# Corner scores and cross-chunk products of a decayed attention: both heads' 128 rows contracted against zeros, in place of 64 rows of each head

## Chip, cores and metric

One core of a Trainium2 chip (8 cores in 2 dies) runs the whole kernel. The metric is the device time of one execution in microseconds, taken as the median of several runs.

## The reference

Attention without softmax, with a decay per head, and then two pairs of dense layers (with a leaky activation in the first, a GELU-like one in the second). Everything is float32.

```
batch, n_heads, seq, head_dim = (4, 8, 576, 64)
...
scores = scale * np.matmul(q, k.transpose(0, 1, 3, 2))
gamma = 1.0 - 2.0 ** (-5.0 - np.arange(H, dtype=np.float32))
rel = pos[:, None] - pos[None, :]
Dmat = np.where(rel >= 0, gamma[:, None, None] ** rel[None, :, :], 0.0)
ret = scores * Dmat[None, :, :, :]
return np.matmul(ret, v).astype(np.float32)
...
x = np.ascontiguousarray(attn_out.transpose(0, 2, 1, 3)).reshape(B * S, H * D)
x = _moe_ref(x=x, **moe_kwargs)        # (max(h, 0) + alpha * min(h, 0)) @ w_out, h = x @ w_in
return _moe2_ref(x=x, **moe2_kwargs)   # (h * sigmoid(1.702 h)) @ w_out
```

## The kernel before, in words

The attention stands at the start and the dense layers fill the rest. A unit of attention is one of 16 pairs `(b, p)`: batch `b` and two heads. The two heads lie above each other in the 128 partitions: head `e = 0` has rows 0 to 63, head `e = 1` rows 64 to 127 (`halves` holds the two slices). The 576 positions are cut into four chunks of 128 and a corner of 64. Scores are computed inside a chunk only; what earlier chunks give to later ones goes through a running 64 x 64 state of each head (a sum of outer products of keys and values), since the decay is a power.

`tc.manual_schedule()` means that each engine executes its instructions in the order in which the code calls them. The loop runs `i` from 0 to 16, and `j = i - 1` is the pair before. What one turn of it puts on TensorE (PE), all through the helper `mm` on line 353, is:

1. `a_scores(i)`, tile `sc`: 8 products that contract 64 rows into 128 columns of the array. `k[j][o]` and `q[j][o]` are one head's rows.
2. `a_outer(i)`, tile `st` from `kts` (keys by position, scaled beforehand by ScalarE in `a_keys`): 8 products that contract 128 rows into 64 columns, the two heads in different columns.
3. `a_within(j)`, tile `av` from `r` and `ld`: 8 products, 128 rows into 64 columns.
4. `a_tail(i)`, tile `st` from `ld`: the corner's scores, 2 products of 64 rows into 64 columns (for `i = 0` they stand between 1 and 2).
5. `a_across(j)`, tile `av`: 8 products of the states with the faded queries and 2 of the corner, 64 rows into 64 columns.

Each float32 product makes two records of a weight load and a matmul, so a group of 8 shows as x16. The trace writes the shape as rows * columns: 64\*128, 128\*64, 64\*64.

The other engines in a turn:

- GpSimd (POOL) multiplies the queries with a fade: `a_queries(i)`, line 400, one 128 x 448 product of two SBUF operands into `r`. A dependency added by hand lets it start only behind the instruction that `latest[0]` names, mostly the last one of `a_sums` (line 424) of the pair before.
- VectorE (DVE): `a_evac(i)`, line 385, two 128 x 512 products that read the scores from PSUM and write `r`; after it, in some turns, tables (line 335, in turns 0 to 2) or work on the dense layers' weights (lines 148, 108, 178) that `run_to` calls by a table of times; then `a_sums(i)`, lines 414, 419, 424, on the states. The last of these writes the masked corner scores back into `r`.
- ScalarE (ACT): `a_states(i)` and `a_keys(i + 1)` on line 317, copies of results (line 103), and weight work (lines 133, 137, 141).
- SyncE (SP) issues the loads: `a_load` (tile `ld`, 128 x 1728 numbers a pair, line 309, and `kts`, line 311) four to five turns ahead, weights (`raw`), stores.

SBUF is cut by hand into slots `w0` to `w15`. `TMP` gives the slots that tiles take in turn: `ld` has five, `r` two, `xs` (results on their way to DRAM) four, `w14` the last of these.

After the loop the first dense layer starts at once: `mm1` (line 514, tile `h`), then `activate`, `split` (ScalarE's and VectorE's halves of `gsf`), `mm2` (line 555, tile `acc`).

## Time and profile before

| | |
|---|---|
| runs | 800.33, 802.6, 804.19 us, median 802.6 |
| profiled execution | 800.28 us, of which the span of the instructions 798.6 |
| busy | PE 793.6 us, DVE 642.1, ACT 527.9, POOL 83.5 |
| granted clock of TensorE | 1.00 in the whole span |
| attention on PE | from 4.5 to 66.5 us of the span |

The profiled execution lies 2.3 us under the median of the runs. The trace gives start and duration of each instruction in us from the span's start, with the idle time ahead of it in brackets and what ended it ("issue" is a pause that no semaphore explains). PEld is the weight load that runs beside the matmuls. A matmul's end is modelled, so what counts on PE is how far apart the starts lie.

### The profile page before, as it was taken

Reading aid. Unit: us, or ns where it says so; the run is one execution under the profiler, and the core shown is the slowest. Engines: PE = TensorE matmul, PEld = TensorE weight load, DVE = VectorE, ACT = ScalarE, POOL = GpSimd, SP = SyncE. Lnnn points to the kernel's source line nnn. Section 1 sums busy time; section 2 is a strip of 40 time slices with the busy share of each in tenths; the row PEclk is TensorE's granted clock in tenths of the full one; section 3 lists DMA queues with packets and bytes.
Section 4 is the critical chain, followed back from the end, with each engine's and each line's share of the span. In section 5 each row is a group of like instructions: output and inputs, shape, how many; then the busy total and the mean of one; then the engine's idle time right before and its main releaser. Section 6 shows DMA issues by size and latency. Waiting matters only on the chain.

```text
span 798.6 us, 14132 instructions
## 1 busy us (share of the span) xinstructions
PE 793.6 (99%) x5004; PEld 740.2 (93%) x5004; DVE 642.1 (80%) x1195; ACT 527.9 (66%) x959; POOL 83.5 (10%) x104
## 2 busy tenths in 40 slices
PE   9999999999999999999999999999999999999998
PEld 8998888888888888999999999999999999999997
DVE  7888987888467576879999899799677898787775
ACT  7689869885536856556678666676566675666552
POOL 2230112100022003626100000000000000000000
PEclk9999999999999999999999999999999999999999
DMA  9998999755889966797989556986435985536771
GB/s 351 417 386 333 327 352 342 286 217 209 294 278 401 360 224 227 253 337 254 337 323 355 177 174 233 343 295 235 147 125 193 323 312 187 159 120 232 267 278 60
DMA packets 87789, 214.08 MB, mean 268 GB/s; under 512 B 7971, under 2 KB 43811, under 8 KB 79014
## 3 DMA queue, kind: packets, MB, share of 16 engines
q1 hardware_dynamic: 80784, 187.99, 65.6%
q0 software_dynamic: 6784, 25.17, 9.0%
q8 instruction: 39, 0.64, 0.3%
q14 instruction: 32, 0.26, 0.1%
q10 hardware_dynamic: 150, 0.02, 0.0%
HBM read 152.59 MB, written 60.56 MB: 267 GB/s over the span
## 4 chain that ended last, share of the span: by engine, by line
PE 98%; DMA 1%; DVE 0%; issue 0%
PE acc L696 33%; PE h L696 25%; PE acc L555 16%; PE h L514 16%; PE av L353 4%; PE sc L353 2%; PE st L353 2%; DMA ws<-sm 1%; PE wps L942 0%; PE dq L326 0%; DVE c L178 0%; DVE wz L930 0%
## 5 line engine op out<-in xcount | busy, mean ns | idle before, releaser
L108 DVE TENSOR_TENSOR gsf<-g,gsf 128x384 fp32r<-128x384 f32 (+1 forms) x272 | 156.4, 586 | 54.5 <-ACT gsf L103 53.1
L103 ACT ACTIVATE gsf<-g 128x384 fp32r<-128x384 f32 (+1 forms) x272 | 145.8, 542 | 75.6 <-PE acc L696 32.8
L555 PE MATMUL acc<-gsf,wo 128*128 128x512 f32 x576 | 138.2, 389 | 0.0
L514 PE MATMUL h<-x,wi 128*128 128x512 f32 x576 | 138.2, 389 | 0.0
L696 PE MATMUL acc<-gsf,ws 128*128 128x384 f32 x768 | 135.1, 334 | 0.2 <-DMA ws<-sm 0.2
L696 PEld LDWEIGHTS acc<-gsf,ws 128*128 128x128 f32 x768 | 133.2, 188 | 0.5 <-ACT x L103 0.5
L555 PEld LDWEIGHTS acc<-gsf,wo 128*128 128x128 f32 x576 | 108.1, 188 | 22.8 <-ACT raw L103 0.3
L514 PEld LDWEIGHTS h<-x,wi 128*128 128x128 f32 x576 | 108.1, 188 | 22.5
L696 PE MATMUL acc<-x,ws 128*128 128x384 f32 x660 | 128.3, 334 | 0.0
L696 PEld LDWEIGHTS acc<-x,ws 128*128 128x128 f32 x660 | 115.5, 188 | 0.2 <-ACT tm L103 0.2
L696 PE MATMUL h<-x,ws 128*128 128x384 f32 x540 | 107.7, 334 | 0.0
L696 PE MATMUL h<-gsf,ws 128*128 128x384 f32 x576 | 101.9, 334 | 0.0
L696 PEld LDWEIGHTS h<-gsf,ws 128*128 128x128 f32 x576 | 100.0, 188 | 0.2 <-issue 0.2
L696 PEld LDWEIGHTS h<-x,ws 128*128 128x128 f32 x540 | 94.8, 188 | 0.0
L178 DVE TENSOR_TENSOR tm<-h,tm 128x384 f32<-128x384 f32 x97 | 53.6, 553 | 26.9 <-PE h L696 21.5
L178 DVE TENSOR_TENSOR g<-g 128x384 f32<-128x384 f32 x114 | 63.0, 553 | 0.7
L103 ACT ACTIVATE tm<-acc 128x384 f32<-128x384 f32 x62 | 30.4, 491 | 48.0 <-PE acc L696 46.4
L522 DVE SCALAR_TENSOR_TENSOR g<-g,rise_sb,h 128x512 f32<-128x512 f32 (+1 forms) x49 | 36.4, 742 | 29.7 <-ACT g L527 29.5
L527 ACT ACTIVATE g<-h 128x512 f32<-128x512 f32 (+1 forms) x49 | 29.1, 593 | 40.5 <-PE h L514 39.9
L178 DVE TENSOR_TENSOR raw<-raw 128x256 f32<-128x256 f32 x116 | 45.6, 433 | 1.0
L148 DVE SCALAR_TENSOR_TENSOR raw<-raw 128x1024 int32<-128x1024 int32 x32 | 39.3, 1229 | 2.6 <-ACT raw L141 2.6
L129 POOL DMA_DIRECT2D raw<-in_w_dram x44 | 23.2, 534 | 173.2 <-DVE raw L178 52.9
(104 smaller groups left out, 922.9 us busy)
## 6 DMA issues: line engine op xcount, KB each, us to landing
ws<-sm SPq DMA_DIRECT2D x32, 1024.0 KB, 7.0
ws<-sp SPq DMA_DIRECT2D x24, 1024.0 KB, 5.5
raw<-in_w_dram POOLq DMA_DIRECT2D x44, 512.0 KB, 7.5
sm<-raw SPq DMA_DIRECT2D x32, 512.0 KB, 4.3
pad<-rg SPq DMA_DIRECT2D x48, 256.0 KB, 2.7
ld<-in_qkv_dram SPq DMA_DIRECT2D x13, 864.0 KB, 7.9
raw<-in_w_dram SPq DMA_DIRECT2D x20, 512.0 KB, 8.9
r<-raw SPq DMA_DIRECT2D x16, 512.0 KB, 2.9
```

Of the source, the lines that this page charges most:

```text
L103: return nc.scalar.activation(out=out, in_=in_, func=ACTF.Copy)
L108: latest[0] = eng.tensor_tensor(out=out, in0=a, in1=b.bitcast(F32), op=ALU.subtract)
L129: eng.dma_start(out=raws[key][:, c * DM:c * DM + DM], in_=f[:, c * DM:c * DM + DM])
L148: latest[0] = nc.vector.scalar_tensor_tensor(out=g[:, 0:2 * DM], in0=t[:, :, 1], scalar=3, in1=t[:, :, 0], op0=ALU.logical_shift_left, op1 ...
L178: latest[0] = (eng or nc.vector).tensor_tensor(out=out, in0=x, in1=y, op=op)
L353: return nc.tensor.matmul(out=out, lhsT=lhsT, rhs=rhs, start=start, stop=stop, skip_group_check=True)
L514: nc.tensor.matmul(out=t, lhsT=w[:, cw, k * 128:k * 128 + 128], rhs=x[:, cx], start=(i == 0), stop=(i == 3 * NK - 1),)
L522: nc.vector.scalar_tensor_tensor(out=g[0], in0=g[1], scalar=rise_sb[:, m:m + 1], in1=h, op0=ALU.mult, op1=ALU.add)
L527: nc.scalar.activation(out=out, in_=in_, func=ACTF.Relu, scale=-1.0)
L555: nc.tensor.matmul(out=acc[0][d], lhsT=w[:, d // 2, cw, d % 2 * 128:d % 2 * 128 + 128], rhs=g[:, cx], start=(m == m0 and i == 0), stop=(m ...
L696: nc.tensor.matmul(out=out, lhsT=w(cw), rhs=x(cx), start=(start and n == 0), stop=True, skip_group_check=True,)
```

## The change

The products of `a_tail` and `a_across` now contract all 128 rows of both heads. One of the two operands has zeros in the other head's rows, so the sum is the same. For that:

- the corner's keys come from the host as 128 columns with zeros (`last`), so `ld` is 128 x 1792 numbers and the loads' cuts shift by 64 columns;
- a fixed tile `rq` in slot `w14` holds the faded queries and the masked corner scores, two buffers of `[128, 2, 512]`; its other-head halves are set to zero once, by two DVE instructions at the start;
- `a_queries` is now two POOL products of 64 partitions each, and the last instruction of `a_sums` two DVE products of 64 partitions each, since each head's half goes to another column range of `rq`;
- the fourth slot of `xs` is `w3` (free of `ld` after pair 11) in place of `w14`.

```diff
-TMP = {"ld": (2, 3, 4, 5, 10), "r": (6, 7), "xs": (11, 12, 13, 14)}
+TMP = {"ld": (2, 3, 4, 5, 10), "r": (6, 7), "xs": (11, 12, 13, 3)}
...
-        t = tmp("ld", i, [128, 1728])
-        cuts = {0: (0, 512, 1152, 1728), 1: (0, 1152, 1728), 2: (0, 1152, 1728)}.get(i, (0, 1728))
+        t = tmp("ld", i, [128, 1792])
+        cuts = {0: (0, 512, 1216, 1792), 1: (0, 1216, 1792), 2: (0, 1216, 1792)}.get(i, (0, 1792))
...
-        k = [t[:, j:j + 128] for j in (128, 256, 832, 960)] + [t[:, 1088:1152]]
-        ld[i] = q, k, t[:, 1152:1728].rearrange("p (n d) -> p n d", n=9), t[:, 384:832]
+        k = [t[:, j:j + 128] for j in (128, 256, 832, 960)]
+        k.append(t[:, 1088:1216].rearrange("p (e n) -> p e n", e=2))
+        ld[i] = q, k, t[:, 1216:1792].rearrange("p (n d) -> p n d", n=9), t[:, 384:832]
...
-        for o in halves:
-            mm(s_t[i][o, 0:64], k[4][o], q[4][o], i == 0, True)
+        for e, o in enumerate(halves):
+            mm(s_t[i][o, 0:64], k[4][:, e], q[4], i == 0, True)
...
-            r[:, 1088:1600].rearrange("p (b n) -> p b n", b=2)[:, :, 0:64], r[:, 1600:2048],
-        )
-        ins = nc.gpsimd.tensor_tensor(
-            out=r_t[i][3], in0=ld[i][3], in1=tab_sb[:, PAIRS[i][1], 320:768], op=ALU.mult
-        )
-        if behind:
-            tc.add_manual_dep(ins.ins, behind.ins.name, SYNC, reason="beside the products of the scores")
+            r[:, 1088:1600].rearrange("p (b n) -> p b n", b=2)[:, :, 0:64], rq[:, i % 2],
+        )
+        for e, o in enumerate(halves):
+            ins = nc.gpsimd.tensor_tensor(
+                out=r_t[i][3][o, e, 0:448], in0=ld[i][3][o], in1=tab_sb[o, PAIRS[i][1], 320:768],
+                op=ALU.mult,
+            )
+            if behind:
+                tc.add_manual_dep(
+                    ins.ins, behind.ins.name, SYNC, reason="beside the products of the scores"
+                )
...
-        latest[0] = nc.vector.tensor_tensor(
-            out=s[:, 0:64], in0=s[:, 0:64], in1=tab_sb[:, p, 256:320], op=ALU.mult
-        )
+        for e, o in enumerate(halves):
+            latest[0] = nc.vector.tensor_tensor(
+                out=r_t[i][3][o, e, 448:512], in0=s[o, 0:64], in1=tab_sb[o, p, 256:320], op=ALU.mult
+            )
...
-            for o in halves:
-                mm(out[c][o], s[o, s0:s0 + 64], q[o, c * 128 - 128:min(c * 128, 448)], False, True)
-        for o in halves:
-            mm(out[4][o], v[o, 8], s[o, 0:64], False, True)
+            for e, o in enumerate(halves):
+                mm(out[c][o], s[:, s0:s0 + 64], q[:, e, c * 128 - 128:min(c * 128, 448)], False, True)
+        for e, o in enumerate(halves):
+            mm(out[4][o], v[:, 8], q[:, e, 448:512], False, True)
...
+        rq = wp.tile([128, 2, 2, 512], F32, tag="w14", name="rq")
+        for e, o in enumerate(halves):
+            nc.vector.memset(rq[o, :, 1 - e], 0.0)
...
+    last = np.zeros((B, NP, 128, 128), np.float32)
+    for e in range(2):
+        o = slice(64 * e, 64 * e + 64)
+        last[:, :, o, o] = kt[:, :, o, 512:]
```

How it moves instructions. On PE, turn 2 of the loop reads before and after as follows (the sizes are those of the output; `sc` are scores, `st` states and corner scores, `av` results):

```order
L353 MATMUL sc<-ld 128x128 x8
L353 MATMUL st<-ld,kts 64x64 x8
L353 MATMUL av<-r,ld 64x128 x8
L353 MATMUL st<-ld 64x64 x2
L353 MATMUL av<-r 64x128 x6
L353 MATMUL av<-r 64x64 x2
L353 MATMUL av<-r,ld 64x64 x2
```

```order
L354 MATMUL sc<-ld 128x128 x8
L354 MATMUL st<-ld,kts 64x64 x8
L354 MATMUL av<-r,ld 64x128 x8
L354 MATMUL st<-ld 64x64 x2
L354 MATMUL av<-rq,r 64x128 x6
L354 MATMUL av<-rq,r 64x64 x2
L354 MATMUL av<-rq,ld 64x64 x2
```

Number, order and output sizes are the same; the last four groups change only what they contract.

On DVE, turns 1 and 2 before and after, each with the semaphores that an instruction waits for:

```order
L385 TENSOR_TENSOR r<-sc,tab_sb 128x512 [waits PE_49] x2
L335 SCALAR_TENSOR_TENSOR tab_sb<-fade_sb,vtab_sb,mask_sb 128x128 x2
L335 SCALAR_TENSOR_TENSOR tab_sb<-fade_sb,vtab_sb,mask_sb 64x64 x2
L414 SCALAR_TENSOR_TENSOR r<-r,vtab_sb 128x192 [waits Activation_49]
L419 SCALAR_TENSOR_TENSOR r<-r,vtab_sb 128x128 [waits DVE_49]
L424 TENSOR_TENSOR r<-r,tab_sb 128x64
L385 TENSOR_TENSOR r<-sc,tab_sb 128x512 [waits PE_49,Pool_49]
L385 TENSOR_TENSOR r<-sc,tab_sb 128x512 [waits PE_49]
```

```order
L386 TENSOR_TENSOR r<-sc,tab_sb 128x512 [waits PE_49] x2
L336 SCALAR_TENSOR_TENSOR tab_sb<-fade_sb,vtab_sb,mask_sb 128x128 x2
L336 SCALAR_TENSOR_TENSOR tab_sb<-fade_sb,vtab_sb,mask_sb 64x64 x2
L419 SCALAR_TENSOR_TENSOR r<-r,vtab_sb 128x192 [waits Activation_49]
L424 SCALAR_TENSOR_TENSOR r<-r,vtab_sb 128x128 [waits DVE_49]
L430 TENSOR_TENSOR rq<-r,tab_sb 64x64 x2
```

One 128 x 64 product has become two of 64 x 64, and the first evacuation no longer waits for POOL, which no longer writes `r`.

On POOL, the queries' products of pairs 2 to 6 before, and of pairs 2 to 4 after:

```order
L400 TENSOR_TENSOR r<-ld,tab_sb 128x448 [waits DVE_49,PE_49,DMAHW1_49,Activation_49,Pool_49]
L400 TENSOR_TENSOR r<-ld,tab_sb 128x448 [waits DVE_49,PE_49,DMAHW4_49,Activation_49,Pool_49]
L400 TENSOR_TENSOR r<-ld,tab_sb 128x448 [waits DVE_49,DMAHW6_49,PE_49,Pool_49]
L400 TENSOR_TENSOR r<-ld,tab_sb 128x448 [waits DVE_49,PE_49,DMAHW1_49,Activation_49,Pool_49]
L400 TENSOR_TENSOR r<-ld,tab_sb 128x448 [waits DVE_49,PE_49,DMAHW3_49,Activation_49,Pool_49]
```

```order
L402 TENSOR_TENSOR rq<-ld,tab_sb 64x448 [waits DVE_49,PE_49,DMAHW1_49,Activation_49,Pool_49]
L402 TENSOR_TENSOR rq<-ld,tab_sb 64x448 [waits PE_49,Pool_49]
L402 TENSOR_TENSOR rq<-ld,tab_sb 64x448 [waits DVE_49,PE_49,DMAHW4_49,Activation_49,Pool_49]
L402 TENSOR_TENSOR rq<-ld,tab_sb 64x448 [waits PE_49,Pool_49]
L402 TENSOR_TENSOR rq<-ld,tab_sb 64x448 [waits DVE_49,DMAHW6_49,PE_49,Pool_49]
L402 TENSOR_TENSOR rq<-ld,tab_sb 64x448 [waits PE_49,Pool_49]
```

Each product has become two; what the second waits for is the use of its half of the buffer two pairs earlier, not the first.

## Rows read from the trace of the kernel before

**Rows 1.** The page: busy time of PE; the chain that ended last, by engine.

```profile
PE 793.6 (99%) x5004; PEld 740.2 (93%) x5004; DVE 642.1 (80%) x1195; ACT 527.9 (66%) x959; POOL 83.5 (10%) x104
...
PE 98%; DMA 1%; DVE 0%; issue 0%
```

**Rows 2.** Waits of 0 to 70 us: total us, times, longest.

```profile
PEld st L353 <- issue: 2.6, 15, 0.2
```

**Rows 3.** PE in turn 12 (timeline: start us, us, shape, xcount).

```profile
49.47 1.16 PE L353 MATMUL sc<-ld 64*128 64x128 f32 x16
...
52.06 0.33 PE L353 MATMUL st<-ld 64*64 64x64 f32 x4
52.22 0.94 PE L353 MATMUL av<-r 64*64 64x128 f32 x16
...
53.21 0.38 PE L353 MATMUL sc<-ld 64*128 64x128 f32 x2
```

**Rows 4.** PE around 51.15 and around 52.05 us alone, same columns.

```profile
50.96 0.29 PE L353 MATMUL st<-ld,kts 128*64 128x64 f32 x4
51.08 0.28 PE L353 MATMUL av<-r,ld 128*64 128x128 f32 x2
...
51.85 0.28 PE L353 MATMUL av<-r,ld 128*64 128x128 f32 x2
52.06 0.27 PE L353 MATMUL st<-ld 64*64 64x64 f32 x1
```

**Rows 5.** DVE and POOL in turn 12, timeline, idle before and its releaser in brackets.

```profile
49.40 0.42 DVE L414 SCALAR_TENSOR_TENSOR r<-r,vtab_sb 128x192 f32<-128x192 f32 x1 [1.11 <-ACT r L317]
...
50.12 0.22 DVE L424 TENSOR_TENSOR r<-r,tab_sb 128x64 f32<-128x64 f32 x1
...
50.60 1.15 POOL L400 TENSOR_TENSOR r<-ld,tab_sb 128x448 f32<-128x448 f32 x1 [2.67 <-DVE r L424]
50.74 1.29 DVE L385 TENSOR_TENSOR r<-sc,tab_sb 128x512 f32<-128x512 f32 x2 [0.39 <-PE sc L353]
...
51.94 1.22 DVE L148 SCALAR_TENSOR_TENSOR raw<-raw 128x1024 int32<-128x1024 int32 x1
```

**Rows 6.** The start: POOL's and DVE's memsets, DVE's tables, POOL's first product.

```profile
0.31 0.10 POOL L1153 MEMSET const-float32-0.0<- 128x1 f32 x1 [0.31 <-issue]
0.34 0.10 POOL L1153 MEMSET const-float32-1.0<- 128x1 f32 x1
...
0.90 0.17 DVE L930 MEMSET wz<- 128x128 f32 x1 [0.90 <-PEq L1153]
...
5.32 1.10 DVE L335 SCALAR_TENSOR_TENSOR tab_sb<-fade_sb,vtab_sb,mask_sb 128x128 f32<-128x128 f32 x4 [4.13 <-ACT fade_sb L103]
...
7.83 1.98 DVE L335 SCALAR_TENSOR_TENSOR tab_sb<-fade_sb,vtab_sb,mask_sb 128x128 f32<-128x128 f32 x4
...
8.22 1.21 POOL L400 TENSOR_TENSOR r<-ld,tab_sb 128x448 f32<-128x448 f32 x1 [6.85 <-ACT tab_sb L103]
...
11.90 1.09 DVE L335 SCALAR_TENSOR_TENSOR tab_sb<-fade_sb,vtab_sb,mask_sb 128x128 f32<-128x128 f32 x4
```

**Rows 7.** Loads: page's issues; busy by stretch (DMA share, GB/s last); turns 3 and 4.

```profile
ld<-in_qkv_dram SPq DMA_DIRECT2D x13, 864.0 KB, 7.9
...
12.00:16.00 4.00, 4.00 (x78) 3.64 (x80) 3.92 (x12) 2.75 (x9) 1.21 (x2) 1.00 1.02 416
...
15.64 1.16 PE L353 MATMUL sc<-ld 64*128 64x128 f32 x16
16.02 0.91 ACT L317 ACTIVATE kts<-kts,vtab_sb 128x256 f32<-128x256 f32 x2 [0.57 <-DMA kts<-in_kn_dram]
...
19.61 1.16 PE L353 MATMUL sc<-ld 64*128 64x128 f32 x16
```

**Rows 8.** Start of the dense layers: the lower half of `gsf`, and the products that use it.

```profile
74.31 0.68 DVE L108 TENSOR_TENSOR gsf<-g,gsf 128x512 fp32r<-128x512 f32 x1
...
74.76 2.94 PE L555 MATMUL acc<-gsf,wo 128*128 128x512 f32 x12
```

More of the change, by code (lines that the diff above doesn't have):

```diff
@@ L1115, in _layout @@
         [
-            qt[..., :128], kt[..., :256], qt[..., 128:], kt[..., 256:], vv, vt,
+            qt[..., :128], kt[..., :256], qt[..., 128:], kt[..., 256:512], last, vv, vt,
         ],
```

## The prediction

> **What bounds the kernel now.** I read the page first, then the waits, then the timeline. TensorE is busy for 793.6 of 798.6 us, and the chain that ended last is 98% TensorE [rows 1]. So time is won only by shortening what TensorE does or by taking out pauses between its instructions, and lost wherever something new comes too late for it. The list of waits holds one entry for TensorE inside the attention that repeats: ahead of the corner scores (`st`) its weight loads stand idle 15 times, 2.6 us together, with no semaphore behind it [rows 2]. That pause comes from the array itself.
>
> The timeline of one turn tells what it is. A turn lasts 53.21 - 49.47 = 3.74 us [rows 3]. Inside a group, instructions come in pairs, one for each head, and two heads share a start. Between the states (128\*64) and the products inside a chunk (128\*64) nothing happens: from 50.96, two pairs of 64 columns take 0.12 us, 0.06 each, and then the next group starts [rows 4]. The last pair of 128 columns starts at 51.85; seven pairs lie between it and 51.08, so a pair takes 0.11 us. But the corner scores (64\*64) start only at 52.06, 0.21 us later: 0.10 us more than a pair needs [rows 4]. Their own two pairs then take 52.22 - 52.06 = 0.16 us where the states' two take 0.12: another 0.04 [rows 3, 4]. So going from 128\*64 to 64\*64 costs TensorE 0.14 us. Where the shape stays, from corner scores to the products across chunks, there is no idle time.
>
> **The change, part by part.**
>
> *The pause.* All that a turn does behind its scores now has the shape 128\*64, so one of its three changes of shape is gone; the ones into and out of the scores (64\*128) stay. It is removed in 17 places: once in each of the 17 turns. All 17 give 17 x 0.14 = 2.4 us; I take fewer, below.
>
> *The products themselves.* Their number, their columns and their weight loads' columns are as before; only rows of zeros are added. The 128\*64 rows show 0.06 us for a pair of 64 columns and 0.11 for 128 [rows 4], and the products across chunks, 64\*64 so far, go at the same pace: six pairs of 0.11 and two of 0.06 make 0.78 us, and their row has 0.94 with the length of the last one [rows 3]. Cost nothing.
>
> *The loads.* `ld` grows from 864 KB a pair [rows 7] by 64 x 4 x 128 bytes = 32 KB, 16 times. In this stretch the DMA engines are full: share 1.02, 416 GB/s [rows 7]. More bytes are therefore later bytes, 0.08 us a pair, 1.3 us by the last. Where that meets TensorE is turn 3: ScalarE stood idle 0.57 us for the keys of that turn, which come last in the queue behind four loads, and turn 3 took 19.61 - 15.64 = 3.97 us instead of 3.74 [rows 7]. Four loads are 131 KB, 0.32 us. So turn 3 comes 0.32 us later, and whatever turns 0 to 2 won is lost in the same wait. Behind turn 3 the distance between landing and use grows, since later loads are issued about four turns ahead (four turns are 15 us) with a median of 7.9 us to landing [rows 7]; I price the rest at nothing, and at 1.3 us if that cover is gone.
>
> *VectorE.* The two memsets of `rq` write 1024 numbers a partition each. One of 128 took 0.17 us [rows 6], so 1.3 us each at the most; they lie in the 4.13 us in which VectorE waits for the tables' input [rows 6]: nothing. The corner scores' masking becomes two instructions in place of one of 0.22 us [rows 5]: 0.22 us more a turn at the most. Cover: in turn 12 VectorE idles 0.39 us and the sums end at 50.34, 1.9 us before the products across chunks start at 52.22 [rows 3, 5]. In turns 1 to 3 VectorE is full (3.92 of 4 us [rows 7]), and it falls 0.7 us behind there at the most, less than the 1.9. Nothing; 16 x 0.22 = 3.5 us if none of it were covered.
>
> *GpSimd.* This is the term with the widest bounds. One product of 128 x 448 took 1.15 us [rows 5]; no row shows one of 64 partitions. It may cost half (0.58) or the same (1.15), and the two may run one after the other or side by side: 1.15 to 2.30 us a turn. It matters because of VectorE. Where a GpSimd product ran beside the tables, which read two operands from SBUF, the four tables took 1.98 us against 1.10 and 1.09 without it [rows 6]. Beside the evacuation, which reads PSUM, nothing was lengthened: 1.29 us with GpSimd on top of it [rows 5]. At 1.15 us the pair stays in the shadow of the evacuation, as now; at 2.30 the second half falls on what follows, in turn 12 an instruction of 1.22 us [rows 5].
> The Trainium skill, "GPSIMD Engine Reference", section "Instruction dispatch", says that each of GpSimd's cores serves 16 partitions and starts the next instruction as soon as its own share of the last is done. By that rule the two halves, on different partitions and with no wait on each other, take about 1.15 us together; in turn they would take 2.30.
> What the rows can say points the same way: two memsets of 0.10 us start 0.03 us apart [rows 6], so GpSimd does begin an instruction before the last has ended. I take 1.15 to 1.3 us, hence no cost, and keep 2.30 as a rival.
>
> *The rest.* ScalarE no longer waits for GpSimd before it writes the states; it waited for TensorE at nearly the same moment, so nothing. The slot change of `xs` moves no work.
>
> **Sum.** Turns 0 to 2: nothing. Turns 3 to 16: 14 x 0.14 = 1.96 us won. Turn 3's load: 0.32 us lost. Net 1.6 us: span 798.6 - 1.6 = 797.0, profiled execution 800.28 - 1.6 = 798.7. That execution lies 2.3 us under the median of 802.6, so the median to expect is 802.6 - 1.6 = **801.0 us**. With all 17 pauses won and no load late it is 800.2; with ScalarE and VectorE, both nearly full in some turns, giving back most, 802.3. That is this case's own range.
>
> **The rivals.**
>
> *A: GpSimd's halves run in turn, and VectorE is the loop.* GpSimd may start only behind the last of the sums. Then a turn is: 0.26 us from the sums' end to GpSimd's start (50.34 to 50.60), 2.30 us of GpSimd, the last half of it holding VectorE up, then the sums, 50.34 - 49.40 = 0.94 us and 0.13 more for the second masking [rows 5]: 3.63 us, just what a turn of TensorE takes without its pause (3.60). Any VectorE work on SBUF in between goes on top: tables of 1.1 us in two turns [rows 6], weight work of 1.2 us or more in six [rows 5]. Eight times 1.15 is 9.2 us; the 1.9 us of distance absorbs some once, and the pauses won in other turns another 1: about 6 us slower. If a half takes only 0.58 us, little of it stays. Price 5 us, **807.6 us**, at most 809.6. It decides from about 1.7 us for the pair. For it: no row shows halves side by side. Against: the memsets.
> The Trainium skill, "SBUF — State Buffer", section "Who interferes with whom", has VectorE with two SBUF inputs fully blocked by a GpSimd instruction that reads SBUF, and the tables' row agrees (0.88 us more beside 1.21). It makes the price of this rival what it is.
>
> *B: the gain is given back.* The first dense layer follows at once, fed by weights that come through the same full queues. The lower half of `gsf` is done at 74.31 + 0.68 = 74.99, and the third product of `acc`, the first to read it, is due at 74.76 + 2 x 2.94 / 12 = 75.25 [rows 8]: 0.26 us to spare. If that chain hangs on loads that cannot move up, TensorE, 1.6 us ahead, waits there for all but 0.26; if the loads are 1.3 us later, it waits longer. Price: 0.3 us faster to 1 us slower, **802.8**. For it: the full DMA and that thin margin. Against: ScalarE and VectorE idle on TensorE at the end of the attention, so their chain moves up with it.
>
> *C: the pause is not one of shape* but of the corner scores (their keys or bank), and stays. Then only the later load is left: 0.3 us slower, **802.9**. Against: the change of shape is the only thing that the paused places share and that the unpaused ones lack.
>
> **How the numbers follow.** Chances: forecast 0.62, A 0.20, B 0.13, C 0.05. What a measurement of this kernel tells from no change is about 0.5%, 4.0 us (its runs lie 3.9 us apart). Faster by that needs more than all 17 pauses give: 0.04, for chance alone. Slower needs A at near its price: 0.16. The same: 0.80. The range for 8 in 10 reaches from 799.4 (all pauses won, and a run a little lower) to 806.5, into A; it leaves out the upper part of A, some 0.13, and 0.05 below.
>
> **What would show it.** Right: in the changed trace the corner scores start 0.11 us behind the last pair before them, the entry of 2.6 us is gone from the waits, a turn takes 3.60 us, the keys' wait of turn 3 grows from 0.57 by about 0.3, and the dense layers start near 64.9 instead of 66.5 us. GpSimd's two products start within some 0.1 us of each other. Wrong: the second product starts where the first ends, VectorE's instructions behind the evacuation grow by up to 1 us, and TensorE waits in `av` for VectorE (A); the first `acc` has a wait of a microsecond (B); the pause ahead of `st` is still there (C).

## The result and the profile after

The changed kernel takes 808.58 us, median of 6 runs (807.62 to 809.04), where the kernel before took 802.05 (800.33 to 804.19) beside it: ratio 1.0077, 95% interval 1.0065 to 1.0089. The forecast was 801.0 with a range up to 806.5, so it was wrong, and the other way: 6.5 us slower. Rival A, priced at 807.6, is nearest, and the three signs that the prediction named for it are in the trace.

The page of the changed kernel, busy times and the chain that ended last, against [rows 1]:

```profile
PE 796.9 (99%) x5004; PEld 742.6 (92%) x5004; DVE 659.9 (82%) x1213; ACT 528.1 (65%) x959; POOL 101.4 (13%) x120
...
PE 89%; DVE 8%; DMA 1%; ACT 1%; issue 0%
```

GpSimd is busy 17.9 us longer, VectorE 17.8, and 8% of the chain, which was 98% TensorE, is now VectorE. The waits of TensorE's weight loads in the first 76 us (total us, times, longest), against [rows 2]:

```profile
PEld av L354 <- DVE r L419: 1.8, 3, 1.1
PEld av L354 <- DVE x L108: 1.7, 1, 1.7
PEld st L354 <- ACT kts L318: 1.6, 3, 0.8
...
PEld st L354 <- issue: 0.2, 1, 0.2
```

The pause ahead of `st` is gone (2.6 us, 15 times, is now 0.2, once). In its place stand waits for VectorE, and on the keys (`kts`) for ScalarE. The timeline of turn 5 on TensorE, one that nothing disturbs, against [rows 3, 4]:

```profile
26.12 0.60 PE L354 MATMUL sc<-ld 64*128 64x128 f32 x6
...
28.17 0.61 PE L354 MATMUL av<-r,ld 128*64 128x128 f32 x8
...
28.60 0.28 PE L354 MATMUL st<-ld 128*64 128x64 f32 x4
28.72 0.94 PE L354 MATMUL av<-rq,r 128*64 128x128 f32 x16
...
29.71 0.38 PE L354 MATMUL sc<-ld 64*128 64x128 f32 x2
```

Four pairs lie between 28.17 and 28.60, 0.11 us each, and the corner scores follow in that step; they take 28.72 - 28.60 = 0.12 us instead of 0.16. The turn lasts 29.71 - 26.12 = 3.59 us, where it was 3.74. That much of the forecast held. Where it went wrong shows in turn 3 (GpSimd, VectorE and TensorE; the brackets of the third row are TensorE's wait):

```profile
16.63 2.35 POOL L402 TENSOR_TENSOR rq<-ld,tab_sb 64x448 f32<-64x448 f32 x2 [2.12 <-ACT r L318]
17.61 2.01 DVE L336 SCALAR_TENSOR_TENSOR tab_sb<-fade_sb,vtab_sb,mask_sb 128x128 f32<-128x128 f32 x4
20.51 1.09 PE L354 MATMUL av<-r,ld 128*64 128x128 f32 x16 [1.59 <-DVE x L108]
```

GpSimd's pair takes 2.35 us in place of one product of 1.15 [rows 5]. Its second half lies on the tables, which take 2.01 us where they took 1.09 with no GpSimd beside them [rows 6] (1.40 in this place of the kernel before, where the end of the single product lay on them), and TensorE, which needs what VectorE does behind them, stands idle 1.59 us. The turn takes 5.84 us, before 3.97 [rows 7]. VectorE near the end of the attention, from one evacuation (L386) to the next, with GpSimd's pair:

```profile
64.40 1.29 DVE L386 TENSOR_TENSOR r<-sc,tab_sb 128x512 f32<-128x512 f32 x2
64.59 2.43 POOL L402 TENSOR_TENSOR rq<-ld,tab_sb 64x448 f32<-64x448 f32 x2 [1.88 <-PE av L354]
65.60 2.38 DVE L178 TENSOR_TENSOR raw<-raw 128x256 f32<-128x256 f32 x4
67.90 0.40 DVE L419 SCALAR_TENSOR_TENSOR r<-r,vtab_sb 128x192 f32<-128x192 f32 x1
...
68.61 0.46 DVE L430 TENSOR_TENSOR rq<-r,tab_sb 64x64 f32<-64x64 f32 x2
69.11 1.29 DVE L386 TENSOR_TENSOR r<-sc,tab_sb 128x512 f32<-128x512 f32 x2
```

and the same kinds of work in the kernel before, in turn 15, the last that has scores:

```profile
61.93 1.29 DVE L385 TENSOR_TENSOR r<-sc,tab_sb 128x512 f32<-128x512 f32 x2
63.14 1.54 DVE L178 TENSOR_TENSOR raw<-raw 128x256 f32<-128x256 f32 x4
64.60 0.41 DVE L414 SCALAR_TENSOR_TENSOR r<-r,vtab_sb 128x192 f32<-128x192 f32 x1
...
65.31 0.22 DVE L424 TENSOR_TENSOR r<-r,tab_sb 128x64 f32<-128x64 f32 x1
65.45 1.22 DVE L148 SCALAR_TENSOR_TENSOR raw<-raw 128x1024 int32<-128x1024 int32 x1
```

VectorE waits for no other engine between these rows, so each starts when the one before lets it. Before, this work takes 65.45 - 61.93 = 3.52 us, within a turn of TensorE. After, it takes 69.11 - 64.40 = 4.71. Of the 1.19 us more, 0.84 come from the sums on the weights (from 65.60 to 67.90 instead of 63.14 to 64.60), which GpSimd keeps out, and 0.36 from the masking (0.50 us to the next row instead of 0.14). VectorE is the loop there: its own work, and no longer TensorE's, sets how long a turn takes.

### The profile page after: what moved, and what is told of

Same layout as the page of the kernel before. It is cut to its first block, busy times and chain, and to the rows that moved or that the text cites. A ratio compares the mean times of both kernels' runs of the same rounds, so it can differ in the third digit from the quotient of the medians.

```text
span 807.0 us, 14160 instructions
## 1 busy us (share of the span) xinstructions
PE 796.9 (99%) x5004; PEld 742.6 (92%) x5004; DVE 659.9 (82%) x1213; ACT 528.1 (65%) x959; POOL 101.4 (13%) x120
## 4 chain that ended last, share of the span: by engine, by line
PE 89%; DVE 8%; DMA 1%; ACT 1%; issue 0%
PE acc L702 32%; PE h L702 24%; PE h L520 16%; PE acc L561 16%; DVE r L386 2%; DVE r L419 1%; DMA ws<-sp 1%; DVE tab_sb L336 1%; DVE r L424 1%; DVE rq L430 1%; DVE x L108 1%; DVE raw L178 1%; DVE raw L148 1%; PE wps L951 0%; DVE wo L108 0%
## 5 line engine op out<-in xcount | busy, mean ns | idle before, releaser
L108 DVE TENSOR_TENSOR gsf<-g,gsf 128x384 fp32r<-128x384 f32 (+1 forms) x272 | 155.9, 585 | 56.1 <-ACT gsf L103 54.9
L402 POOL TENSOR_TENSOR rq<-ld,tab_sb 64x448 f32<-64x448 f32 x32 | 38.1, 1192 | 32.2 <-ACT tab_sb L103 8.2
```

The source lines that it names most:

```text
L108: latest[0] = eng.tensor_tensor(out=out, in0=a, in1=b.bitcast(F32), op=ALU.subtract)
L402: ins = nc.gpsimd.tensor_tensor(out=r_t[i][3][o, e, 0:448], in0=ld[i][3][o], in1=tab_sb[o, PAIRS[i][1], 320:768], op=ALU.mult,)
```

## The experiments

The table has each kernel's median, its ratio to the kernel before as measured in the same series (802.05 us beside the changed kernel, 801.4 to 801.5 beside the others), and from its trace the time from the start of turn 1 to the first product of the dense layers. Kernels of different series are best compared by their ratios. Turn 0 is left out of the last column because it varies by more than a microsecond in a way that does not follow the changes: turn 1 starts at 9.05 in the profile of before, 10.11 in that of the changed kernel, 10.29 in masks_alone, where only the masking is cut, and 9.19 in after_one_mask, which has all of the change but the second masking.

| kernel | us | ratio, 95% interval | turn 1 to dense layers |
|---|---|---|---|
| before | 801.4 | | 57.4 |
| changed | 808.58 | 1.0077 [1.0065, 1.0089] | 64.0 |
| before_two_halves | 805.59 | 1.0051 [1.0038, 1.0064] | 62.1 |
| masks_alone | 801.72 | 1.0004 [0.9993, 1.0014] | 57.8 |
| halves_and_masks | 808.82 | 1.0094 [1.0080, 1.0108] | 65.0 |
| before_loads | 802.34 | 1.0010 [1.0001, 1.0019] | 58.4 |
| shapes_only | 800.46 | 0.9987 [0.9978, 0.9995] | 55.2 |
| all_but_products | 808.00 | 1.0083 [1.0071, 1.0096] | 64.6 |
| after_one_product | 800.89 | 0.9997 [0.9988, 1.0005] | 57.5 |
| after_one_mask | 804.43 | 1.0038 [1.0024, 1.0052] | 61.7 |
| whole_and_half | 802.07 | 1.0016 [1.0007, 1.0024] | 58.6 |
| whole_and_whole | 805.13 | 1.0047 [1.0034, 1.0061] | 61.7 |
| half_on_vector | 806.74 | 1.0066 [1.0050, 1.0082] | 62.1 |
| padded_states | 806.90 | 1.0069 [1.0055, 1.0083] | 63.0 |
| padded_keys_first | 805.73 | 1.0053 [1.0041, 1.0065] | 62.3 |

**GpSimd's product alone** (before_two_halves)

```diff
-        ins = nc.gpsimd.tensor_tensor(
-            out=r_t[i][3], in0=ld[i][3], in1=tab_sb[:, PAIRS[i][1], 320:768], op=ALU.mult
-        )
...
+        for o in halves:
+            ins = nc.gpsimd.tensor_tensor(
+                out=r_t[i][3][o], in0=ld[i][3][o], in1=tab_sb[o, PAIRS[i][1], 320:768], op=ALU.mult
+            )
...
```

> The kernel before, with only GpSimd's product cut into two of 64 partitions each, written to the same columns of `r`. Theory 1 (the two halves cost GpSimd twice the time and hold VectorE up): each half takes about 1.14 us, the pair 2.3, VectorE's instructions on SBUF that fall beside the second half grow by up to 1 us, and the kernel is 6 to 10 us slower than before, at 808 to 812 us; the changed kernel's 6.5 us are then this cost less the pauses won. Rival (longer loads, products over rows of zeros, the other slot of `xs`, or the second masking make the changed kernel slow): nothing of that is in here, so within 1 us of the kernel before.

Measured: 4.1 us slower. That is less than the 6 to 10 expected, but no other part is in it. The second half waits for no semaphore in this program, and the pair still takes twice the time (GpSimd, and VectorE near the end, against the row of 1.54 above):

```profile
24.31 2.35 POOL L401 TENSOR_TENSOR r<-ld,tab_sb 64x448 f32<-64x448 f32 x2 [0.97 <-DVE r L427]
...
63.16 2.85 DVE L178 TENSOR_TENSOR raw<-raw 128x256 f32<-128x256 f32 x4
```

**The changed kernel without it** (after_one_product)

```diff
-        for e, o in enumerate(halves):
-            ins = nc.gpsimd.tensor_tensor(
-                out=r_t[i][3][o, e, 0:448], in0=ld[i][3][o], in1=tab_sb[o, PAIRS[i][1], 320:768],
-                op=ALU.mult,
-            )
...
+        ins = nc.gpsimd.tensor_tensor(
+            out=r_t[i][3][:, 0, 0:448], in0=ld[i][3], in1=tab_sb[:, PAIRS[i][1], 320:768], op=ALU.mult
+        )
...
-                mm(out[c][o], s[:, s0:s0 + 64], q[:, e, c * 128 - 128:min(c * 128, 448)], False, True)
+                mm(out[c][o], s[:, s0:s0 + 64], q[:, 0, c * 128 - 128:min(c * 128, 448)], False, True)
```

> The changed kernel with GpSimd's product as one instruction of 128 partitions again, into the first of the two column ranges of `rq`, which the products across chunks then read for both heads. It leaves out the zeros, so the two heads' results are mixed; all else, the products' number and shape too, is as in the changed kernel. Theory 1: 17 pauses of 0.15 us are won and little is lost, 2 us faster than before, 799.5 to 801.5 us. Rival (longer loads, the other slot, the second masking or the products themselves): it stays near the changed kernel, 806 to 809 us.

Measured: 800.89 us. All of the loss is gone with the pair. But only 0.6 us of the 2.5 is left as a gain, and its interval includes no change. Turns 2, 3 and 10 take 4.15, 4.05 and 4.74 us (before 3.73, 3.97 and 3.73), most of the others 3.59. In turn 3 ScalarE waits for the load of the keys, 1.33 us where it was 0.57 [rows 7]; in turn 10 it waits for a weight's load ahead of the keys, which it does not do in the kernel before, and TensorE for the keys (timeline of ScalarE):

```profile
16.72 0.91 ACT L318 ACTIVATE kts<-kts,vtab_sb 128x256 f32<-128x256 f32 x2 [1.33 <-DMA kts<-in_kn_dram]
...
41.49 1.18 ACT L133 ACTIVATE raw<-raw 128x1024 f32<-128x1024 f32 x1 [0.86 <-DMA raw<-in_w_dram]
```

and over the whole attention the weight loads' wait on the keys is

```profile
PEld st L354 <- ACT kts L318: 1.8, 5, 0.9
```

**The loads alone** (before_loads)

```diff
-        t = tmp("ld", i, [128, 1728])
+        t = tmp("ld", i, [128, 1792])
...
-            qt[..., :128], kt[..., :256], qt[..., 128:], kt[..., 256:], vv, vt,
+            qt[..., :128], kt[..., :256], qt[..., 128:], kt[..., 256:], kt[..., 512:], vv, vt,
```

> The kernel before with only the loads of the changed kernel: 128 x 1792 numbers a pair instead of 1728, the 64 new columns unused. The prediction's term: the keys' wait of turn 3 grows by 0.32 us and nothing else, 0.3 us slower. Theory 1: no more than that. Rival (later loads are what costs): 3 us slower or more, with waits on DMA.

Measured: 0.8 us slower (0.1 to 1.5 by the interval): more than the 0.3 of the prediction, if anything, and far from the 6.5. Part of it shows in turn 10, which takes 4.11 us instead of 3.73; ScalarE waits for a weight's load there too:

```profile
42.56 1.17 ACT L133 ACTIVATE raw<-raw 128x1024 f32<-128x1024 f32 x1 [0.53 <-DMA raw<-in_w_dram]
```

In shapes_only below, where the loads are as before, turn 10 starts at nearly the same time as in after_one_product (41.87 and 41.68 us), ScalarE does not wait, and the turn takes 3.64 us. So this wait goes with the longer loads.

**The shape alone** (shapes_only)

```diff
-            mm(s_t[i][o, 0:64], k[4][o], q[4][o], i == 0, True)
+            mm(s_t[i][o, 0:64], k[4], q[4], i == 0, True)
...
-                mm(out[c][o], s[o, s0:s0 + 64], q[o, c * 128 - 128:min(c * 128, 448)], False, True)
+                mm(out[c][o], s[:, s0:s0 + 64], q[:, c * 128 - 128:min(c * 128, 448)], False, True)
...
```

> The kernel before with nothing changed but the products' shape: corner scores and products across chunks contract all 128 rows of what lies there, without zeros, so the two heads' results are mixed; loads, GpSimd and VectorE are as before. The pauses alone are 17 x 0.145 = 2.5 us. If all of it reaches the end, 799 us where the kernel before has 801.5. If the loads, which are full in this stretch, or ScalarE and VectorE take it back at the start of the dense layers (rival B of the prediction), 800.5 to 801.5 us, with a wait on a weight's DMA or on their work in its place.

Measured: 0.9 us faster (0.4 to 1.8). From turn 1 on the attention is 57.4 - 55.2 = 2.2 us shorter, as 16 pauses of 0.14 make. How much of that is lost further on, the two profiles do not tell, since turn 0 took 1.09 us longer in this one (5.62 us against 4.53); that leaves 1.15 us of lead at the start of the dense layers. That start loses nothing (from the first product to the first of `acc` it is 8.30 us, as in the kernel before), so it is not rival B's place. Of the 1.15 us, 0.4 are left at the end, and in the second half of the kernel TensorE waits for a weight's load (waits behind the attention):

```profile
PE h L696 <- DMA ws<-sp: 0.6, 1, 0.6
```

The only such row of the kernel before has 0.2 us.

**Everything but the shape** (all_but_products)

```diff
-            out=r_t[i][3], in0=ld[i][3], in1=tab_sb[:, PAIRS[i][1], 320:768], op=ALU.mult
+                out=r_t[i][3][o], in0=ld[i][3][o], in1=tab_sb[o, PAIRS[i][1], 320:768], op=ALU.mult
...
-            out=s[:, 0:64], in0=s[:, 0:64], in1=tab_sb[:, p, 256:320], op=ALU.mult
+                out=s[o, 0:64], in0=s[o, 0:64], in1=tab_sb[o, p, 256:320], op=ALU.mult
```

(each in a loop over the halves, and the loads of 1792 columns)

> Everything of the change on GpSimd, VectorE and in the loads, and nothing on TensorE: the kernel before with loads of 1792 columns, GpSimd's product in two halves and the masking in two, all three groups of products of the old shape. It tells what the changed shape is worth beside GpSimd's pair. If TensorE's pauses are won there too, it is 2 us slower than the changed kernel (810 to 811 us). If VectorE and GpSimd are the loop, so that TensorE's pauses only turn into waits, it is as fast as the changed kernel or faster: the cut product alone cost 4.1 us and the loads alone 0.8, so 806 to 808 us.

Measured: 808.0 us, which can't be told from the changed kernel (ratios 1.0083 and 1.0077, with overlapping intervals). From turn 1 to the dense layers it takes 64.6 us against 64.0. With VectorE as the loop in the slow turns, next to nothing is left of the pauses won on TensorE.

**Halves and maskings** (halves_and_masks, masks_alone, after_one_mask)

> The kernel before with GpSimd's product in two halves and the masking in two, with the old loads and shapes. The halves alone cost 4.1 us, and halves, maskings and loads together 6.6. If the second masking (0.25 us of VectorE a turn) costs what VectorE's fullness lets it, 6 us slower than before: it is 0.25 us in the turns where VectorE is the loop, some eight, so 2 us more than the halves alone. If the rest is the loads', 4 to 4.5 us slower.

The edit is that of the last kernel without the loads. Measured: 7.4 us slower, 3.3 more than with the halves alone, although the prediction had priced the second masking at nothing. Of the next two kernels, masks_alone does the masking alone, and after_one_mask undoes it in the changed kernel (its edit):

```diff
-        for e, o in enumerate(halves):
-            latest[0] = nc.vector.tensor_tensor(
-                out=r_t[i][3][o, e, 448:512], in0=s[o, 0:64], in1=tab_sb[o, p, 256:320], op=ALU.mult
-            )
+        latest[0] = nc.vector.tensor_tensor(
+            out=r_t[i][3][:, 0, 448:512], in0=s[:, 0:64], in1=tab_sb[:, p, 256:320], op=ALU.mult
+        )
...
```

> The kernel before with nothing but the masking in two instructions. If 0.36 us a turn of VectorE is covered as long as VectorE is not the loop, as the prediction had it: within 0.5 us of the kernel before (some of it in turn 3 and the last turns, where VectorE is nearly full). If the masking is a cost of its own: 2 to 3 us slower.

> The changed kernel with the masking of the corner scores in one instruction of 128 partitions, into the first column range, which the corner's product then reads for both heads: it leaves out the zeros there, so the heads' corners are mixed. All else, GpSimd's two halves too, is as in the changed kernel. In the kernel with halves and two maskings, the evacuation starts 0.50 us behind the first masking, against 0.13 us with one: 0.36 us a turn, in the nine turns or so in which VectorE is the loop, 3.2 us. If so, 3 to 4 us faster than the changed kernel: 804.5 to 805.5 us. Rival (halves and maskings cost 3.3 us by chance of that one kernel's order): within 1 us of the changed kernel.

Measured: 0.3 us slower alone, which can't be told from nothing. Undone in the changed kernel, it gives 804.43 us: by the ratios (1.0038 and 1.0077) 3.1 us faster, by the medians of the two series 4.15. So the masking is covered while VectorE has time to spare and is paid beside the halves, where it has none. The rows of VectorE in turn 1, first with halves and one masking, then with halves and two:

```profile
11.52 0.22 DVE L427 TENSOR_TENSOR r<-r,tab_sb 128x64 f32<-128x64 f32 x1
11.66 1.28 DVE L385 TENSOR_TENSOR r<-sc,tab_sb 128x512 f32<-128x512 f32 x2
```

```profile
11.56 0.46 DVE L428 TENSOR_TENSOR r<-r,tab_sb 64x64 f32<-64x64 f32 x2
12.05 1.29 DVE L385 TENSOR_TENSOR r<-sc,tab_sb 128x512 f32<-128x512 f32 x2
```

The evacuation starts 0.14 us behind the masking in the one and 0.49 behind it in the other.

**How much GpSimd, or how late the queries?** (whole_and_half, whole_and_whole)

```diff
+        nc.gpsimd.tensor_tensor(
+            out=spare, in0=ld[i][3][:, 0:224], in1=tab_sb[:, PAIRS[i][1], 320:544], op=ALU.mult
+        )
...
```

(`spare` lies in slot `w14`, so both kernels also have the changed kernel's other slot for `xs`)

> The kernel before with a second GpSimd product of 128 x 224 behind that of the queries, from the same operands into a spare tile that nobody reads: 1.14 + 0.62 = 1.76 us of GpSimd a turn, the queries no later than before. The prediction's rival A decides from about 1.7 us: less than 1 us slower. If the cost goes with the time that GpSimd keeps VectorE out (4.1 us for 1.15 us more), 0.62 us more cost 2.2 us.

> The same with a second product of 128 x 448 into the spare tile: 2.3 us of GpSimd a turn, as much as the two halves, but the queries of both heads are ready as early as before. Theory 1 (the time in which VectorE is kept out): as slow as with the two halves, 3.5 to 4.5 us above the kernel before. Rival (what costs is that the upper head's queries come 1.15 us later to the products across chunks): within 0.5 us of the kernel before.

Measured: 0.7 us slower with 224 columns more, 3.8 us with 448 (which gives `spare` 448 columns too). So what costs is not that the upper head's queries come late, since nobody reads the spare tile and 448 columns cost nearly as much as the halves (4.1). Nor is it the other slot of `xs`: with it and 224 columns more, the loss is 0.7 us in all. And it is not in proportion: the first 0.6 us of GpSimd cost 0.7 us, the next 0.5 cost 3.1 more. That fits rival A's point of about 1.7 us a turn.

**The second half on VectorE** (half_on_vector)

```diff
+    def a_half(i):
+        o = halves[1]
+        latest[0] = nc.vector.tensor_tensor(
+            out=r_t[i][3][o, 1, 0:448], in0=ld[i][3][o], in1=tab_sb[o, PAIRS[i][1], 320:768], op=ALU.mult
+        )
...
```

> The changed kernel with the upper head's half of the queries' product on VectorE, behind the sums, and only the lower one on GpSimd. VectorE gets an instruction of 64 x 448 a turn, about 0.6 us by its 128 x 448 and 128 x 512 subtractions (0.61 and 0.68 us), and loses the 1.15 us in which the second half on GpSimd kept it out. Theory 1 (what costs is the time in which GpSimd keeps VectorE out, not VectorE's own work): 3 to 6 us faster than the changed kernel, 802 to 805 us. Rival (VectorE is simply full, whoever does the half): 807 us or more.

Measured: 806.74 us, worse than theory 1 said and just under the rival's bound. By the ratios (1.0066 and 1.0077, with overlapping intervals) it can't be told from the changed kernel, though the attention from turn 1 on is 1.9 us shorter (62.1 against 64.0). The half takes VectorE 0.62 us where on GpSimd it kept VectorE out for 1.15, and TensorE now waits for that instruction (waits of the weight loads):

```profile
PEld av L354 <- DVE rq L413: 4.6, 5, 2.2
```

In its full turns VectorE has no 0.6 us to give either, so its own work counts as well as the time in which it is kept out.

Part of the 806.74 us is something else, the clock. The profile by stretches has first how long TensorE was busy, and third from the end its granted clock:

```profile
66.00:71.00 5.00, 2.53 (x40) 1.90 (x40) 4.85 (x13) 3.35 (x4) 1.13 (x1) 1.00 1.01 410
...
72.00:75.00 3.00, 3.00 (x8) 2.42 (x8) 1.44 (x3) 2.93 (x4) 0.00 (x0) 0.50 0.16 61
```

Behind a stretch in which TensorE stood idle for half of the time, waiting for VectorE, its clock is at the lower level, 0.50 (1.2 of 2.4 GHz), from 72 to 75.4 us. The first products of the dense layers up to the first of `acc` take 9.90 us instead of 8.30, so this costs 1.6 us. Five of the six executions list a mean clock of 0.998 (806.37 to 808.40 us), the sixth lists 1.00 and took 805.15. Without it the kernel would be at about 805.1 us, an estimate from these rows, at the edge of theory 1's range.

**The zeros in the states** (padded_states, padded_keys_first)

```diff
-        scale(s[:, 0:320], s_t.pop(i)[:, 0:320], vtab_sb[:, p, 2:3])
+        s, t = r_t[i][1], s_t.pop(i)
+        for e, o in enumerate(halves):
+            scale(s[o, e, 0:320], t[o, 0:320], vtab_sb[o, p, 2:3])
...
-                mm(out[c][o], s[:, s0:s0 + 64], q[:, e, c * 128 - 128:min(c * 128, 448)], False, True)
+                mm(out[c][o], s[:, e, s0:s0 + 64], q[:, c * 128 - 128:min(c * 128, 448)], False, True)
...
```

> The changed kernel with the zeros in the states instead of in the queries: GpSimd's product is one instruction of 128 partitions into `r` as before; ScalarE writes the states by two instructions of 64 partitions into a tile with fixed zeros, and VectorE's three instructions on them run over both heads' column ranges (384, 256 and 128 columns instead of 192, 128 and 64). Theory 1: GpSimd's pair is gone, so no instruction of VectorE grows by a microsecond; the pauses give 2.5 us; ScalarE has 0.5 us more work a turn, which costs something in the three turns in which it was full (3.70 of 3.73 us): 800 to 802.5 us. Rival (products over zeros or longer loads are what costs): 806 us or more.

```diff
+            if i + 1 < n_a:
+                a_keys(i + 1)
             if 0 < i < n_a:
                 a_tail(i)
                 a_states(i)
...
-            if i + 1 < n_a:
-                a_keys(i + 1)
```

> The kernel with zeros in the states (GpSimd's product whole, ScalarE writing two halves), with one more edit: ScalarE scales the keys of the next pair ahead of writing the states, instead of behind. In the version without this edit each turn took 3.76 to 3.87 us, and TensorE waited for the keys 12 times: the chain corner scores, states (1.07 us), keys (0.91 us), next outer products was the loop. If that is so, turns come down to 3.59 us and the kernel to 800 to 802 us, as with GpSimd's product whole and mixed. Rival (the padded work on VectorE or the products over zeros are the loop): 805 us or more.

Measured: 806.9 and 805.7 us; both expectations fell. GpSimd's pair is gone, but now ScalarE's two instructions (1.07 us where one of 128 partitions took 0.52) come too late. In the first kernel the keys behind them are late, in the second, with the keys ahead, the states themselves (waits of the weight loads, one row of each):

```profile
PEld st L354 <- ACT kts L318: 4.5, 9, 1.1
```

```profile
PEld st L354 <- ACT sz L318: 6.6, 9, 1.8
```

No version with the new shape and all of its zeros is faster than the kernel before. What the shape alone gives is 0.9 us, and the zeros cost more in each of the three ways in which they were made: queries by GpSimd, queries by GpSimd and VectorE, states by ScalarE.

**GpSimd and VectorE by themselves** (pool_bench, vector_bench)

The kernel is a row of instructions, `nc.gpsimd.tensor_tensor(out=t[o, i], in0=u[o, 0:n], in1=v[o, 0:n], op=ALU.mult)` with the partitions `o` and columns `n` of each name, and then VectorE's kinds alone and beside two such products.

> No attention and no dense layers, only GpSimd and VectorE on tiles of their own: the output is filled with zeros, and its total time says nothing. GpSimd alone, without waits between the instructions: products of 128 x 448, of 64 x 448 on the lower and the upper 64 partitions in turn, on the same 64 partitions, of 32 x 448 on all four quarters, of 128 x 224 and of 128 x 896. Theory 1: the time goes by columns alone and the instructions follow one another, 1.14 us for 128, 64 or 32 partitions, 0.6 for 224 columns, 2.3 for 896. Rival (halves on different partitions overlap where no semaphore keeps them apart): a pair starts within 0.1 us and takes 1.2 us. Then VectorE alone and beside two GpSimd products, with 128 x 128 instructions on two SBUF operands, 128 x 512 with one operand in PSUM, and 128 x 128 with one SBUF operand: theory 1 has the first kind stand still for the whole of the GpSimd products (up to 2.3 us for one of 0.28), and the second unchanged; of the third it says nothing.

```profile
3.08 4.39 POOL L35 TENSOR_TENSOR whole<-u,v 128x448 f32<-128x448 f32 x4 [2.64 <-DVE v L28]
...
7.43 7.03 POOL L35 TENSOR_TENSOR twohalves<-u,v 64x448 f32<-64x448 f32 x6
...
14.52 4.37 POOL L35 TENSOR_TENSOR samehalf<-u,v 64x448 f32<-64x448 f32 x4
18.86 4.65 POOL L35 TENSOR_TENSOR quarters<-u,v 32x448 f32<-32x448 f32 x4
23.59 2.50 POOL L35 TENSOR_TENSOR short<-u,v 128x224 f32<-128x224 f32 x4
...
30.17 4.29 DVE L48 SCALAR_TENSOR_TENSOR sums_alone<-long,k,y 128x128 f32<-128x128 f32 x16 [22.02 <-POOL long L35]
...
35.29 6.13 DVE L48 SCALAR_TENSOR_TENSOR sums_beside<-x,k,y 128x128 f32<-128x128 f32 x16
35.33 2.26 POOL L70 TENSOR_TENSOR sums_pool<-u,x 128x448 f32<-128x448 f32 x2 [5.19 <-DVE x L76]
...
42.75 4.87 DVE L56 TENSOR_TENSOR evac_alone<-ps,sums_next 128x512 f32<-128x512 f32 x8
...
48.45 4.87 DVE L56 TENSOR_TENSOR evac_beside<-ps,x 128x512 f32<-128x512 f32 x8
...
54.48 2.25 DVE L62 TENSOR_SCALAR single_alone<-evac_next 128x128 f32<-128x128 f32 x16
...
57.56 4.14 DVE L62 TENSOR_SCALAR single_beside<-x 128x128 f32<-128x128 f32 x16
```

From the first start of a row to the first of the next, a product of 448 columns takes (7.43 - 3.08) / 4 = 1.09 us on 128 partitions, (18.86 - 14.52) / 4 = 1.09 on the same 64, and (23.59 - 18.86) / 4 = 1.18 on 32, a new quarter each time: the columns set it. Lower and upper halves in turn take (14.52 - 7.43) / 6 = 1.18 each, one behind the other. Beside 2.26 us of GpSimd, VectorE's sums on two SBUF operands take 1.84 us longer and its evacuations nothing.

> No attention and no dense layers, the output filled with zeros; VectorE alone, products of two SBUF operands without waits between them: 64 columns of 128 partitions, of the same 64, of the lower and upper 64 in turn; 448 columns of 128 and of halves; 128 and 64 partitions in turn. By the kernels, an instruction behind one of 128 partitions starts 0.08 us before that one's end, and behind one of 64 partitions 0.03 us after it. If that goes with the partitions, the starts lie 0.13 us apart for 128 partitions and 0.24 for 64, whichever half. If it goes with the other things around it there, they lie equally far apart.

```profile
8.06 1.10 DVE L35 TENSOR_TENSOR whole<-u,v 128x64 f32<-128x64 f32 x8
9.08 0.19 DVE L36 COPY x<-y 128x64 f32<-128x64 f32 x1
9.18 1.16 DVE L35 TENSOR_TENSOR samehalf<-u,v 64x64 f32<-64x64 f32 x8
10.27 0.18 DVE L36 COPY x<-y 128x64 f32<-128x64 f32 x1
10.37 1.84 DVE L35 TENSOR_TENSOR twohalves<-u,v 64x64 f32<-64x64 f32 x8
12.24 0.20 DVE L36 COPY x<-y 128x64 f32<-128x64 f32 x1
```

An instruction takes (9.08 - 8.06) / 8 = 0.13 us on 128 partitions and (10.27 - 9.18) / 8 = 0.14 on the same 64 again and again, but (12.24 - 10.37) / 8 = 0.23 when the halves change. The first alternative of the expectation, that it goes with the number of partitions, is wrong: it goes with the change from one half to the other. Two more rows of this kernel agree: 128 partitions and the lower 64 in turn, which start at the same partition, take 0.14 us each, and of 448 columns an instruction takes 0.54 us on 128 partitions and 0.64 when the halves change.

## Why the prediction was wrong

**The step that failed** is "I take 1.15 to 1.3 us, hence no cost, and keep 2.30 as a rival". The pair takes 2.35 us. The row behind the choice, two memsets 0.03 us apart [rows 6], is of instructions with one column; it says nothing of products of 448. The Trainium skill, "GPSIMD Engine Reference", section "Instruction dispatch", was read as if cores without partitions in an instruction went on to the next at once. Here the halves follow one another and each costs a whole, in each kernel that has them and by themselves (1.18 us from start to start); the measurement decides. Whether the idle cores still walk through the instruction, no run here shows.

**What follows from it** came as rival A had it. VectorE's instructions with two SBUF operands are kept out, those that read one of them from PSUM are not (pool_bench: 6.13 against 4.29 us, and 4.87 against 4.87). The Trainium skill, "SBUF — State Buffer", section "Who interferes with whom", has it so, and also says that `tensor_scalar`, in a mode that uses two ports, can contend with GpSimd; a `tensor_scalar` with one SBUF operand did (4.14 against 2.25 us). So the pair is covered for the 1.29 us of the evacuation, and in turns 4 to 8 also by the subtraction that reads `av` (L108 on `x`). What is left there lengthens the first of the sums, which takes 0.83 to 1.03 us instead of 0.42, and the pauses that VectorE had pay for that: these turns still take 3.59 us. Where VectorE had weight work or tables as well, the turn grows. From turn to turn the changed kernel loses 1.9 us in turn 3, 0.3 in turn 9, 1.4 in turn 10, 0.4 in turn 14 and 3.6 from the start of turn 15 to the dense layers, and wins 0.14 to 0.16 in most of the others. Cutting the product alone costs 4.1 us; putting it back in the changed kernel wins all of the loss.

**The second masking** was sized at 0.22 us at the most and held to be covered. It takes 0.36, and with the pair beside it it is not covered: 3.3 us by halves_and_masks, 3.1 to 4.15 by after_one_mask. Alone it costs nothing that can be measured. So more than the size, the sum was at fault: each cover was taken from the kernel before, where the other cost is not. Halves alone 4.1 and masking alone 0.3 make 7.4 together. That rival A's 807.6 comes so near to 808.58 is therefore partly luck: it priced the pair at 5 us, which alone cost 4.1, and put next to nothing on the masking.

**The pause** was right in cause and size (0.145 us a turn, predicted 0.14), and rival C is out. What it is worth at the end was not: 2.2 us from turn 1 on are worth 0.9 by the medians when nothing else is changed, and in the changed kernel nothing that can be told from none (all_but_products). Rival B was right that some is given back, but not where: the start of the dense layers loses nothing, and the one profile of shapes_only shows a wait for a later load of weights.

**The loads** cost 0.8 us alone, 0.3 predicted. The keys' wait of turn 3, named as their place, did not show in the changed kernel, where TensorE is late itself by then; in after_one_product it grew from 0.57 to 1.33 us. The loads behind turn 3, priced at nothing, do cost: the wait for a weight's load makes turn 10 last 4.11 us in before_loads and 4.74 in after_one_product instead of 3.73.

**Left open**: what makes turn 0 take between 4.5 and 5.8 us, and with it how much of shapes_only's 2.2 us goes there and how much at the later load; each kernel has one trace only.

## What to carry to other kernels

An instruction cut by partitions cost its engine twice or more here, though it moved the same numbers (GpSimd 2.35 us for 1.15, ScalarE 1.07 for 0.52, VectorE's masking 0.49 for 0.14 to the next start). So splitting one to reach another layout must be paid for in engine time. Before two small costs are called covered, put both into the same engine's turn and add: the cover is one, and it can be spent once. A pause taken out of the busiest engine is worth only as much as what comes next, here VectorE's turn and the loads, can follow.

## What was not expected of the hardware

- A change of the half on which VectorE or GpSimd works costs about 0.10 us: 0.23 us against 0.14 between starts on VectorE, 1.18 against 1.09 on GpSimd. The instruction itself lasts as long, to 0.01 us; it is the overlap with the next that is lost.
- VectorE's `tensor_scalar` with a single SBUF operand stood still beside GpSimd just as the sums with two did: 1.89 us longer beside 2.25 us of GpSimd.
- Behind a stretch of waits TensorE's granted clock fell to 0.50 for 3.4 us in half_on_vector, which cost 1.6 us on top of the waits.
